# Projecting seven heads of the second batch in float32r passes, with the splits on GpSimd

## The chip, the core and the metric

The program runs on one core of a Trainium2 chip. The metric is the device time of one execution in microseconds. Engines are named as the profile names them: PE is TensorE's matmul, PEld its weight load, DVE is VectorE, ACT is ScalarE, POOL is GpSimd, SP is SyncE, which issues the transfers.

## The reference

A random-feature attention ("performer") over 4 batches, 8 heads, 576 positions and 64 channels is followed by two feed-forward layers on 2304 tokens (512 to 2048 to 512):

```python
proj = np.einsum('bhsd,md->bhsm', x, omega)     # x = q or k, scaled; 128 features
sq = np.sum(x * x, axis=-1, keepdims=True) / 2.0
h = proj - sq
h = h - np.max(h, axis=-1, keepdims=True)
phi = np.exp(h) / np.sqrt(m)
...
kv = np.einsum('bhsm,bhsd->bhmd', k_p, v);  z = np.sum(k_p, axis=2)
num = np.einsum('bhsm,bhmd->bhsd', q_p, kv);  den = np.einsum('bhsm,bhm->bhs', q_p, z)[..., None] + 1e-06
...
h = x @ w_in;  g = h * np.clip(h + 3.0, 0.0, 6.0) / 6.0;  x = g @ w_out      # layer 1
h = x @ w_in;  g = h / (1.0 + np.exp(-1.702 * h));        out = g @ w_out    # layer 2
```

All of it is float32 at the boundary. The first step of the attention, proj, is what the change is about.

## The kernel before, in words

The attention of batch 0 runs alone at the start (to about 45 us). Then layer 1 goes through the batches in four loops of 16 chunks (a chunk is 128 of the 2048 hidden columns): `emit_h` (L506) computes the hidden chunk of one batch, ScalarE and VectorE gate it (L517, L518) and split it (L522, L523), and `emit_o` (L556) multiplies it into the output two chunks later. While batch n goes through its chunks, the attention of batch n+1 is worked in step by step: `att_steps` makes a list of steps, and `side()` takes from it four times in a chunk, at every second call, so that the list is empty at the loop's end. Layer 2 follows from about 560 us (L872, L1003).

Products in layer 1 and 2 are made of float32r passes: an operand is split into a rounded part (hi) and the rest (lo), and three passes hi*hi, hi*lo, lo*hi add up. For a projection this is `project` (L261): `T(h)` splits a head's keys and queries into thi and tlo (L318 a copy, L319 a subtraction, each 128x512, two buffers of either), and `PJ(h, j)` runs 6 passes of 256 columns for the keys (j = 0) and for the queries (j = 1). omega stands in a block-diagonal form in bd_hi and bd_lo, which `factors()` fills with eight small VectorE operations (L699 to L707). The other form is `PJH(h)` (L256): native float32 matmuls of 64 rows and 128 columns on omt, without a split, 8 calls for a head, in two row halves that write two PSUM banks. A flag, `halves`, chooses: before, batches 0 and 1 use PJH (and `PLH` for the 64 positions left over of each head), batches 2 and 3 use T and PJ (and TL, PL). Both forms end in `features`: a maximum over the features on VectorE (L267, from PSUM) and four exponentials on ScalarE (L269). `KV`, `QT`, `NU` and `XT` do the rest of a head on TensorE (L358, L380, L394, L432).

In the first loop (batch 0 in the chunks, batch 1 in the attention) the weights of layer 1 are converted too, one chunk at a time, from the 64-bit words in which they arrive: ScalarE L183 and L185, VectorE L187, L191, L195, GpSimd L200 (two products of 128x512), VectorE L207 (two sums), then the split into hi and lo, ScalarE L210 and VectorE L211. wtop, wmag and wpow, the tiles between these steps, have one buffer each here. The conversion of layer 2's weights follows in the later loops.

The order of the instructions on each engine is made by a scheduler when the program is built: it takes the earliest step of the program that is ready in its own model of time, so an operation that has no one to wait for can come long before its place in the program. On the chip each engine keeps that order.

Of the kernel before, what the change touches and what calls it, by code (L numbers as in the profile page):

```python
# [8 lines left out]
F32 = mybir.dt.float32  # L9
# [6 lines left out]
ALU = mybir.AluOpType  # L16
# [6 lines left out]
def performer_moe_kernel(  # L23
# [13 lines left out]
    nc = tc.nc  # L37
# [5 lines left out]
    H = 2 * NPAIR  # L43
# [60 lines left out]
    def load_pair(b, i):  # L104
        a = at.tile([P, 2, 2, 2, P], F32, tag="qk", bufs=2, name="qk")
        vv = at.tile([P, 2, R, D + 1], F32, tag="v", bufs=2, name="v")
        if (b, i) == (0, 0):
            nc.sync.dma_start(out=a[:, 0], in_=qk[b, i, :, 0])
            nc.sync.dma_start(out=omt, in_=omega)
            load_left(b)  # L110
            nc.sync.dma_start(out=a[:, 1], in_=qk[b, i, :, 1])
        else:
            nc.sync.dma_start(out=a, in_=qk[b, i])
        last_load[0] = nc.sync.dma_start(out=vv, in_=v[b, i])
        qkv[b, i] = (a, vv)

    def load_left(b):
        a = at.tile([P, NPAIR, P], F32, tag="lqk", bufs=1, name="lqk")
        vl = at.tile([P, NPAIR, D + 1], F32, tag="lv", bufs=2, name="lv")
        nc.sync.dma_start(out=a, in_=lqk[b])  # L120
        nc.sync.dma_start(out=vl, in_=lv[b])
        lqkv[b] = (a, vl)
# [31 lines left out]
    def fetch_w(l, k_, c):  # L154
        s = ws_tile(k_, c)
        nc.sync.dma_start(out=s.bitcast(F32), in_=ws_dram[l, k_, c])
        ws[l, k_, c] = s
# [116 lines left out]
    class Att:  # L274


        def __init__(self, b, x, xl, halves=False):
            self.halves = halves
            self.b, self.x, self.xl = b, x, xl
            self.t, self.e, self.kv, self.xt, self.feat, self.qt = {}, {}, {}, {}, {}, {}  # L280

# [33 lines left out]
            self.xln = at.tile([SL, NPAIR, 2, D], F32, tag="xln", name="xln")  # L315

        def split_in(self, hi, lo, a):
            nc.vector.tensor_copy(hi, a)  # L318
            nc.vector.tensor_tensor(out=lo, in0=a, in1=hi.bitcast(F32), op=ALU.subtract)  # L319

        def T(self, h):
            a = qkv[self.b, h // 2][0][:, h % 2]
# [24 lines left out]

        def feature(self, h, j, r):
            e = self.e[h]
            return e[:, r % 2, 2 * j + r // 2] if self.halves else e[:, j, r]  # L350

        def KV(self, h):
            i, p0 = h // 2, 64 * (h % 2)
# [90 lines left out]

    def att_steps(a):
        b = a.b
        st = [] if a.halves else [lambda: a.T(0)]
        for h in range(H + 2):
            if h < H and a.halves:
                st.append(lambda h=h: a.PJH(h))  # L450
            elif h < H:
                st.append(lambda h=h: a.PJ(h, 0))
                st.append(lambda h=h: a.PJ(h, 1))
                if h + 1 < H:
                    st.append(lambda h=h: a.T(h + 1))
            if h == 0:
                st.append(lambda: a.PLH() if a.halves else a.TL())
            if h <= 1 and not a.halves:
                st.append(lambda h=h: a.PL(h))
            if h == 2:  # L460
                st.append(lambda: a.QTL())
            if 2 <= h:
                st.append(lambda h=h: a.NU(h - 2))
            if 1 <= h <= H:
                st.append(lambda h=h: a.QT(h - 1))
                st.append(lambda h=h: a.KV(h - 1))
                if h % 2 == 0:
                    st.append(("load", (h - 1) // 2))
            if 2 <= h and h % 2:
                st.append(lambda h=h: a.XT((h - 2) // 2))  # L470
        st.append(lambda: a.XTL())
        fin = []
        for s in st:
            if isinstance(s, tuple):
                i = s[1] + 2
                bb, i = b + i // NPAIR, i % NPAIR
                if bb < B:
                    prev = fin.pop()

                    def f(prev=prev, bb=bb, i=i):  # L480
                        prev()
                        load_pair(bb, i)
                        if i == 0:
                            load_left(bb)
                    fin.append(f)
            else:
                fin.append(s)
        return fin
# [4 lines left out]
    xblk = {}  # L493
# [96 lines left out]
    def split_x(t, x, kk, eng=nc.gpsimd):  # L590
        nc.scalar.copy(x[:, 0, kk, :], t[:, kk, :])
        eng.tensor_tensor(
            out=x[:, 1, kk, :], in0=t[:, kk, :], in1=x[:, 0, kk, :].bitcast(F32), op=ALU.subtract
        )

    def new_x(i):
        if i == B:
            return lp.tile([P, 2, NK, B * SL], F32R, tag="xl2", name="xl2")
        return xp_.tile([P, 2, NK, SM], F32R, tag="x", bufs=2, name=f"x{i}")
# [85 lines left out]
    for n in range(WARM):  # L685
        nc.tensor.matmul(
            out=ps.rearrange("p a m -> p (a m)"),
# [6 lines left out]
    def factors():  # L694
        for e in range(2):
            o0 = 64 * e
            rows = slice(o0, o0 + 64)
            oth = slice(64 - o0, 128 - o0)
            nc.vector.tensor_copy(bd_hi[rows, e, :], omt[rows, :])  # L699
            nc.vector.tensor_tensor(  # L700
                out=bd_lo[rows, e, :],
                in0=omt[rows, :],
                in1=bd_hi[rows, e, :].bitcast(F32),
                op=ALU.subtract,
            )
            nc.vector.tensor_copy(bd_hi[oth, e, :], zero_r[oth, :].bitcast(F32))
            nc.vector.tensor_copy(bd_lo[oth, e, :], zero_r[oth, :].bitcast(F32))  # L707

    xl = xp_.tile([P, NK, B * SL], F32, tag="xl", name="xl")
    conv = [(l, c) for l in range(2) for c in range(NC)]  # L710
    n_load = [0]
# [2 lines left out]
    def convert_next(stage, upto, act=None, dve=None):  # L714

        while n_conv[stage - 1] < min(upto, len(conv)):
            if stage == 1:
                prefetch_w()
                convert_1(*conv[n_conv[0]], act, dve)
            else:  # L720
                convert_next(1, n_conv[1] + 1, act, dve)
                convert_2(*conv[n_conv[1]])
            n_conv[stage - 1] += 1
        prefetch_w()
# [24 lines left out]
    def before_chunk(n, c):  # L749
        n_late[1] = min(len(late), -(-len(late) * ((n - 1) * NC + c + 1) // slots))  # L750
        late_at("chunk")

    xblk[0] = new_x(0)
    att = Att(0, xblk[0], xl, True)
    steps = att_steps(att)
    for i, st in enumerate(steps):
        if i == len(steps) - TAIL:
# [63 lines left out]
    for u in range(len(units) + LAG):  # L821
        while fetches and fetches[0][0] <= u + AHEAD:
            fetch_w(0, *fetches.pop(0)[1:])
        if u < len(units):
            n, c = units[u]
            if c == 0 and n + 1 < B:
                xblk[n + 1] = new_x(n + 1)
                if n == 1:
                    factors()
                steps = att_steps(Att(n + 1, xblk[n + 1], xl, n == 0))  # L830
                todo = steps[::-1]
                pace[:] = len(todo), 0
            if (n, c) == (B - 2, NC - 1):
                while todo:
                    todo.pop()()
                actx.close()
                lp = ctx.enter_context(
                    tc.tile_pool(name="lp", bufs=1, side="right", reuse_waits="tile")
                )
                xblk[B] = new_x(B)  # L840
                for kk in range(NK):
                    split_x(xl, xblk[B], kk)
            if n > 0:
                before_chunk(n, c)
            emit_h(n, c, side)
            if n == 0:
                convert_next(2, min(c + 2, NC), *(att.feat[H - 1] if c == 0 else ()))
            if (n, c) == (B - 1, PREP):
                assert n_late[0] == len(late)
                prep, _ = x_ops(0, wp, "w")  # L850
            if c == NC - 1:
                while todo:
                    todo.pop()()
        if u >= LAG:
            emit_o(*units[u - LAG], side)
# [343 lines left out]
```

## Time and profile before

| | |
|---|---|
| median of 3 runs | 930.9 us (930.24 to 930.96) |
| the profiled execution | 930.89 us, span 929.1 us |
| PE busy | 914.1 us (98%) |
| DVE busy | 585.9 us (63%) |
| ACT busy | 481.5 us (52%) |
| POOL busy | 334.4 us (36%) |
| TensorE clock granted | 1.0 throughout |

Durations below are those of the profiled execution. Its span counts from the first to the last instruction; 1.8 us of the execution lie around it. The shares are means over stages: in the first loop (36 to 178 us) DVE is much busier than its 63%. Matmuls are pipelined, so the cost of a run of matmuls is read from its first start to the start of what comes next.

### The profile page before, as it was taken

How to read it: one execution, taken by the hardware profiler on the slowest of the kernel's cores; microseconds unless marked ns; L12 is line 12 of the kernel's file. 1: busy time of each engine (PE TensorE's matmuls, PEld its weight loads, DVE VectorE, ACT ScalarE, POOL GpSimd, SP SyncE). 2: the span in 40 equal slices, each digit the busy share in tenths (PEclk: the TensorE clock that was granted, in tenths of full speed). 3: DMA queues.
4: the chain of work that ended last, by engine and by line, in shares of the span. 5: the costliest groups of instructions: out<-in, count | busy, mean ns of one | idle time of the engine just before them, and what ended most of it. 6: DMA issues, size and time to landing. Idle time of an engine off the chain costs nothing.

```text
span 929.1 us, 16457 instructions
## 1 busy us (share of the span) xinstructions
PE 914.1 (98%) x6274; PEld 782.1 (84%) x6274; DVE 585.9 (63%) x980; ACT 481.5 (52%) x977; POOL 334.4 (36%) x283
## 2 busy tenths in 40 slices
PE   8999999999999999999999999999999999999998
PEld 6877777778887888878888888878999888899997
DVE  5888889587585766727643433766875443377653
ACT  6977676476665665636533333444544223244443
POOL 0122222077573547544772112784000244420000
PEclk9999999999999999999999999999999999999999
DMA  6677777889878887766765426999889654566672
GB/s 210 241 250 250 238 248 268 293 297 339 307 271 277 287 319 288 261 238 234 265 239 191 137 93 224 369 405 316 275 285 333 199 175 159 176 187 183 169 261 92
DMA packets 75167, 228.77 MB, mean 246 GB/s; under 512 B 7504, under 2 KB 13264, under 8 KB 75088
## 3 DMA queue, kind: packets, MB, share of 16 engines
q1 hardware_dynamic: 74928, 227.45, 71.2%
q8 instruction: 50, 0.82, 0.3%
q10 hardware_dynamic: 160, 0.26, 0.1%
q14 instruction: 29, 0.24, 0.1%
HBM read 164.77 MB, written 62.91 MB: 245 GB/s over the span
## 4 chain that ended last, share of the span: by engine, by line
PE 84%; DVE 9%; ACT 3%; POOL 2%; issue 1%; DMA 1%; POOLq 0%; DVEq 0%; ACTq 0%
PE o L1003 19%; PE ps L506 18%; PE o L556 18%; PE h L872 16%; PE ps L261 3%; PE hl L889 2%; DVE w L207 2%; PE ps L394 1%; PE ps L256 1%; PE ps L358 1%; DVE gs L523 1%; PE ps L380 1%; POOL w L200 1%; DVE wtop L191 1%; ACT e L269 1%
## 5 line engine op out<-in xcount | busy, mean ns | idle before, releaser
L506 PE MATMUL ps<-x,wss 128*128 128x512 f32 x768 | 193.9, 397 | 3.3 <-ACT wss L210 1.8
L1003 PE MATMUL o<-wss,gs 128*128 128x256 f32 x1536 | 185.4, 283 | 0.3
L1003 PEld LDWEIGHTS o<-wss,gs 128*128 128x128 f32 x1536 | 184.6, 191 | 1.2 <-DVE gs L974 0.5
L506 PEld LDWEIGHTS ps<-x,wss 128*128 128x128 f32 x768 | 139.4, 188 | 35.4 <-ACT wss L210 3.7
L872 PE MATMUL h<-xo,wss 128*128 128x512 f32 x672 | 160.0, 394 | 0.4 <-DVE t L905 0.4
L200 POOL TENSOR_TENSOR w<-w,wpow 128x512 f32<-128x512 f32 x64 | 78.1, 1240 | 202.1 <-DVE wpow L195 123.6
L872 PEld LDWEIGHTS h<-xo,wss 128*128 128x128 f32 x672 | 124.1, 188 | 28.1 <-DVE t L905 0.8
L913 POOL TENSOR_TENSOR g<-g,c 128x512 f32<-128x512 f32 x48 | 64.5, 1346 | 170.3 <-ACT g L912 170.0
L973 ACT CAST gs<-g 128x512 fp32r<-128x512 f32 x112 | 69.4, 621 | 85.1 <-PE o L1003 79.3
L556 PE MATMUL o<-gs,wsh 128*128 128x512 f32 (+1 forms) x480 | 111.7, 377 | 0.3 <-ACT gs L522 0.3
L556 PE MATMUL o<-gs,wss 128*128 128x512 f32 (+1 forms) x480 | 109.4, 374 | 2.4 <-ACT gs L522 2.4
L974 DVE TENSOR_TENSOR gs<-g,gs 128x512 fp32r<-128x512 f32 x112 | 79.7, 716 | 47.8 <-ACT gs L973 45.0
L224 POOL TENSOR_TENSOR wsn<-w,wsn 128x512 fp32r<-128x512 f32 x64 | 90.5, 1429 | 48.8 <-ACT wsn L223 48.8
L518 DVE SCALAR_TENSOR_TENSOR ga<-ga,ps 128x512 f32<-128x512 f32 (+1 forms) x80 | 50.0, 629 | 91.3 <-ACT ga L517 91.1
L517 ACT ACTIVATE ga<-ps,three 128x512 f32<-128x512 f32 (+1 forms) x80 | 51.6, 650 | 94.1 <-PE ps L506 93.9
L556 PEld LDWEIGHTS o<-gs,wss 128*128 128x128 f32 x480 | 81.5, 188 | 17.3 <-ACT gs L522 3.3
L556 PEld LDWEIGHTS o<-gs,wsh 128*128 128x128 f32 x480 | 81.7, 188 | 16.2 <-ACT gs L522 1.0
L269 ACT ACTIVATE e<-ps,mx 128x128 f32<-128x128 f32 x220 | 62.2, 392 | 30.9 <-DVE mx L267 30.9
L523 DVE TENSOR_TENSOR gs<-ga,gs 128x512 fp32r<-128x512 f32 (+1 forms) x80 | 65.1, 824 | 19.4 <-ACT gs L522 18.1
L207 DVE TENSOR_TENSOR w<-w,wtop 128x512 f32<-128x512 f32 x64 | 65.5, 1033 | 10.6 <-POOL w L200 10.2
L912 ACT ACTIVATE g<-c 128x512 f32<-128x512 f32 x48 | 30.3, 632 | 60.3 <-DVE c L905 60.3
L223 ACT CAST wsn<-w 128x512 fp32r<-128x512 f32 x64 | 38.6, 626 | 27.3 <-issue 9.5
(146 smaller groups left out, 1184.1 us busy)
## 6 DMA issues: line engine op xcount, KB each, us to landing
wss<-left SPq DMA_DIRECT2D x64, 512.0 KB, 4.0
wss<-ws0i SPq DMA_DIRECT2D x48, 512.0 KB, 4.6
wraw<-in_w_in_dram SPq DMA_DIRECT2D x32, 512.0 KB, 4.8
wraw<-in_w_out_dram SPq DMA_DIRECT2D x32, 512.0 KB, 5.9
left<-wsn SPq DMA_DIRECT2D x32, 512.0 KB, 3.6
wss<-ws0o SPq DMA_DIRECT2D x24, 512.0 KB, 4.4
ws0i<-wss SPq DMA_DIRECT2D x16, 512.0 KB, 3.1
wss<-sumsa SPq DMA_DIRECT2D x16, 512.0 KB, 3.9
```

What stands on the lines that cost most here:

```text
L200: nc.gpsimd.tensor_tensor(out=w[:, cols], in0=w[:, cols], in1=q[:, cols], op=ALU.mult)
L207: nc.vector.tensor_tensor(out=wj, in0=wj, in1=a[:, j * DM:(j + 1) * DM], op=ALU.add)
L224: nc.gpsimd.tensor_tensor(out=s[:, :, 1], in0=t, in1=s[:, :, 0].bitcast(F32), op=ALU.subtract)
L269: act = nc.scalar.activation(out=e[:, r, :], in_=ps[:, r, :], func=AF.Exp, bias=mx[:, r:r + 1])
L506: nc.tensor.matmul(out=ps, lhsT=w[:, wi, kk, :], rhs=x[:, xi, kk, :], start=(m == 0), stop=(m == 3 * NK - 1),)
L523: gate[1] = nc.vector.tensor_tensor(out=s[:, 1, :], in0=g, in1=s[:, 0, :].bitcast(F32), op=ALU.subtract)
L556: nc.tensor.matmul(out=ps[:, e, :], lhsT=w[:, wi, cols], rhs=s[:, gi, :], start=(c == 0 and m == 0 and per == 1), stop=(c == NC - 1 and m ...
L872: nc.tensor.matmul(out=ps, lhsT=s[:, wi, q, :], rhs=xop[q, op][:, xi], start=(first and m == 0), stop=(m == 5), skip_group_check=not first,)
L913: mul = eng.tensor_tensor(out=g, in0=g, in1=src, op=ALU.mult)
L973: split_ins[0] = nc.scalar.copy(s[:, 0], g)
L974: split_ins[1] = nc.vector.tensor_tensor(out=s[:, 1], in0=g, in1=s[:, 0].bitcast(F32), op=ALU.subtract)
L1003: last_row[0] = nc.tensor.matmul(out=out, lhsT=s[:, gi, d * P:(d + 1) * P], rhs=w[:, wi, :], start=(start and m == 0), stop=(stop and m == 2),
```

## The change

`Att` gets a number, `native`, in place of the flag: so many of its heads use the native form. Batch 0 has all 8, batch 1 has 1 (head 0, and the left-over positions by `PLH` as before), batches 2 and 3 have none, as before. For batch 1 the splits of heads 1 to 7 go to GpSimd; for batches 2 and 3 they stay on VectorE. Since batch 1 now needs bd_hi and bd_lo, `factors()` is called right after omt is scaled and no longer at the start of the second loop. T(h+1) stands in the list of steps behind the projection of head h. Batch 1's list grows from 39 to 53 steps, which `side()` spreads over the same loop.

```diff
-        def __init__(self, b, x, xl, halves=False):
-            self.halves = halves
+        def __init__(self, b, x, xl, native=0, split=None):
+            self.native = native
+            self.split = split or nc.vector
+            self.halves = native > 0
...
         def split_in(self, hi, lo, a):
-            nc.vector.tensor_copy(hi, a)
-            nc.vector.tensor_tensor(out=lo, in0=a, in1=hi.bitcast(F32), op=ALU.subtract)
+            self.split.tensor_copy(hi, a)
+            self.split.tensor_tensor(out=lo, in0=a, in1=hi.bitcast(F32), op=ALU.subtract)
...
         def feature(self, h, j, r):
             e = self.e[h]
-            return e[:, r % 2, 2 * j + r // 2] if self.halves else e[:, j, r]
+            return e[:, r % 2, 2 * j + r // 2] if h < self.native else e[:, j, r]
...
-        st = [] if a.halves else [lambda: a.T(0)]
+        st = [] if a.native else [lambda: a.T(0)]
         for h in range(H + 2):
-            if h < H and a.halves:
+            if h < a.native:
                 st.append(lambda h=h: a.PJH(h))
             elif h < H:
                 st.append(lambda h=h: a.PJ(h, 0))
                 st.append(lambda h=h: a.PJ(h, 1))
-                if h + 1 < H:
-                    st.append(lambda h=h: a.T(h + 1))
+            if a.native <= h + 1 < H:
+                st.append(lambda h=h: a.T(h + 1))
...
+    factors()
+
     xl = xp_.tile([P, NK, B * SL], F32, tag="xl", name="xl")
...
-    att = Att(0, xblk[0], xl, True)
+    att = Att(0, xblk[0], xl, H)
...
-                if n == 1:
-                    factors()
-                steps = att_steps(Att(n + 1, xblk[n + 1], xl, n == 0))
+                steps = att_steps(Att(n + 1, xblk[n + 1], xl, 1 - n if n < 1 else 0, nc.gpsimd if n == 0 else None))
```

## Rows read from the trace of the kernel before

**Rows 1.** Stretches: us, busy time (x instructions) by engine, clock, DMA share, GB/s

```profile
58.00:167.00 109.00, 104.14 (x739) 79.74 (x738) 94.83 (x167) 75.94 (x145) 29.70 (x26) 1.00 0.73 251
...
188.00:313.00 125.00, 124.00 (x853) 100.49 (x852) 90.20 (x149) 76.43 (x171) 76.28 (x65) 1.00 0.85 301
...
313.00:430.00 117.00, 116.87 (x813) 94.39 (x812) 69.06 (x121) 69.34 (x152) 66.29 (x60) 1.00 0.73 255
```

**Rows 2.** Waits, 58 to 167 us: who waits for whom, us, times, longest

```profile
POOL w L200 <- DVE wpow L195: 61.4, 10, 8.2
...
PEld o L556 <- ACT gs L522: 4.3, 6, 1.4
...
PEld ps L506 <- ACT wss L210: 3.4, 4, 1.6
```

**Rows 3.** Timeline, POOL: start, us, engine, line, operation, tiles, count, [idle before]

```profile
103.51 2.30 POOL L200 TENSOR_TENSOR w<-w,wpow 128x512 f32<-128x512 f32 x2 [7.02 <-DVE den L416]
...
110.86 2.28 POOL L200 TENSOR_TENSOR w<-w,wpow 128x512 f32<-128x512 f32 x2 [5.05 <-DVE wpow L195]
...
121.31 2.27 POOL L200 TENSOR_TENSOR w<-w,wpow 128x512 f32<-128x512 f32 x2 [8.18 <-DVE wpow L195]
```

**Rows 4.** Timeline of DVE in the first loop

```profile
104.47 0.69 DVE L518 SCALAR_TENSOR_TENSOR ga<-ga,ps 128x512 f32<-128x512 f32 x1 [0.36 <-ACT ga L517]
...
112.06 1.63 DVE L207 TENSOR_TENSOR w<-w,wtop 128x512 f32<-128x512 f32 x1 [1.34 <-POOL w L200]
...
114.20 0.68 DVE L207 TENSOR_TENSOR w<-w,wtop 128x512 f32<-128x512 f32 x1
```

**Rows 5.** Timeline of PE, native projection of heads 3 and 4, batch 1

```profile
81.88 1.71 PE L256 MATMUL ps<-omt,qk 64*128 64x128 f32 x16
...
83.51 2.57 PE L506 MATMUL ps<-x,wss 128*128 128x512 f32 x10
...
98.41 1.16 PE L256 MATMUL ps<-omt,qk 64*128 64x128 f32 x16
...
99.50 0.68 PE L394 MATMUL ps<-kv,qpt 128*64 128x65 f32 x14
```

**Rows 6.** Timeline of PE, float32r projection of one head, batch 2

```profile
213.47 0.39 PE L261 MATMUL ps<-bd_hi,thi 128*128 128x256 f32 x1
...
214.28 2.91 PE L556 MATMUL o<-gs,wss 128*128 128x512 f32 x12
...
217.03 0.28 PE L261 MATMUL ps<-bd_hi,thi 128*128 128x256 f32 x1
...
217.73 2.91 PE L506 MATMUL ps<-x,wss 128*128 128x512 f32 x12
```

**Rows 7.** Line L224: durations min/median/max in ns, first and last start, form

```profile
L224 POOL TENSOR_TENSOR wsn<-w,wsn x64: 1273/1297/1792, 196.7 to 491.1; 128x512 fp32r<-128x512 f32 x64
```

**Rows 8.** Groups on POOL: busy us, mean ns of one, idle before

```profile
masks.py:199 POOL TENSOR_SCALAR_AFFINE_SELECT ident<-ident 128x128 f32<-128x128 f32 x1 | 0.3, 292 | 0.0
...
masks.py:197 POOL MEMSET ident<- 128x128 f32 x1 | 0.2, 204 | 0.3 <-POOLq L1186 0.3
...
L78 POOL MEMSET three<- 128x1 f32 x1 | 0.1, 99 | 0.0
```

**Rows 9.** Groups on DVE, 36 to 167 us, columns as in rows 8

```profile
L523 DVE TENSOR_TENSOR gs<-ga,gs 128x512 fp32r<-128x512 f32 x14 | 9.4, 680 | 0.0
...
L187 DVE TENSOR_SCALAR wmag<-wtop 128x512 int32<-128x512 int32 x15 | 6.3, 419 | 2.8 <-ACT wtop L183 2.8
```

**Rows 10.** Groups on DVE, 188 to 430 us

```profile
L523 DVE TENSOR_TENSOR gs<-ga,gs 128x512 fp32r<-128x512 f32 x31 | 30.5, 984 | 11.4 <-ACT gs L522 11.3
...
L187 DVE TENSOR_SCALAR wmag<-wtop 128x512 int32<-128x512 int32 x13 | 9.2, 711 | 2.1 <-ACT wtop L183 1.9
```

**Rows 11.** Timeline at the start

```profile
3.93 0.47 DVE L699 CAST bd_hi<-omt 64x128 fp32r<-64x128 f32 x2
```

**Rows 12.** Timeline of ACT in the first loop

```profile
101.69 2.17 ACT L269 ACTIVATE e<-ps,mx 128x128 f32<-128x128 f32 x8
```

## The prediction

> **What bounds the kernel now.** I read first the stretches by stage, then the waits of the first chunk loop, then the order of each engine in it. In the stretch in which batch 0 goes through the chunks (58 to 167 us) TensorE is busy 104.14 of 109 us, so it stands idle for 4.9 us; in the next two loops together it is idle for 1.1 of 242 us [rows 1]. The first loop is thus the one place where TensorE still waits, and the change lies in it. Who makes it wait: the gate's product (L522) and the converted weights (L210, behind L207) [rows 2]. GpSimd's waits say why: in this loop it is nearly always waiting for VectorE's wpow (L195), 61.4 us in 10 waits [rows 2]. The conversion of a chunk's weights is a ring: ScalarE L183, VectorE L187, L191, L195, two GpSimd products L200, two sums L207, and then the next chunk's L183, since wtop, wmag and wpow have one buffer each. Two rounds of it took 103.51 to 110.86 and 110.86 to 121.31 us [rows 3]: the short one has no features in it, the long one has two maxima (L267) and what follows a head. One head falls to about two chunks. In the ring VectorE stops only for the first L200 (1.34 us) [rows 4]. So this loop is held by VectorE's order with the GpSimd step in it, and TensorE comes close behind.
>
> **TensorE: seven projections in another form.** Removed: PJH of heads 1 to 7 of batch 1, 8 calls each, which the trace shows as 16 matmuls. Head 3 took 81.88 to 83.51 = 1.63 us, head 4 took 98.41 to 99.50 = 1.09 us [rows 5]: where the two row halves alternate on the array they run together, otherwise one after the other. By the same view (two of the seven stand there) heads 1 to 7 took some 1.8, 1.50, 1.63, 1.09, 1.09, 1.71 and 1.09, together 9.9 us. Added: PJ, 12 passes of 256 columns for each head; batch 2 shows it in two parts, 213.47 to 214.28 and 217.03 to 217.73, together 1.51 us [rows 6], for seven heads 10.6 us. The sum is +0.7 us; the bounds are 10.6 - 7 x 1.71 = -1.4 us and 10.6 - 7 x 1.09 = +3.0 us. The stage waits for the ring, so I take 0 of it.
> The Trainium skill ("FP8 and Floating Point Precision", TensorE Precision Notes) counts true float32 as four passes through the array. By it a native head would be 8 x 128 x 4 = 4096 columns against 12 x 256 = 3072 of the float32r form, so a quarter of the work would go, an estimate of 0.4 us for each head and 2.9 us in all. Head 4 with its 1.09 us does not bear that out: the two halves overlap there [rows 5].
>
> **GpSimd: seven splits.** T(1) to T(7) each add a copy and a subtraction of 128x512 on GpSimd. The subtraction is the form of L224: 1.27 us at least, 1.30 median [rows 7]. No copy of that size stands in the trace. Upwards, four times the affine select of 128x128 (0.292) gives 1.17 us; downwards, a memset grows from 0.099 for one column to 0.204 for 128, which is 0.52 us at 512 [rows 8]. I take the middle, 0.85. One split is then 2.15 us, seven are 15.0 us (12.6 to 17.3).
> The Trainium skill ("GPSIMD Engine Reference", 3.1 Elementwise) gives 769 ns for a 512-element loop with one input; the sum by it would be 14.4 us.
> GpSimd has room: it is busy 29.70 of 109 us [rows 1]. thi and tlo have two buffers, so a split runs a head ahead of its projection and TensorE does not wait for it (0; a whole split, 2.15 us for each head, if that cover fails).
>
> **What the splits do to VectorE.** This is the term that decides. The first L207 stands beside the second L200 and takes 1.63 us, the second stands alone and takes 0.68 [rows 4]; beside other GpSimd work L523 and L187 grow in the same manner [rows 9, 10], while an operation that reads PSUM keeps its time (L518 at 104.47, 0.69 us beside the pair of 103.51) [rows 3, 4]. So each GpSimd operation that reads SBUF can hold up a VectorE operation with both sides in SBUF until it ends. The price: from 188 to 430 us six groups of this kind (L523, L207, L191, L319, L318, L187) took 33.1 us longer than the same forms in the first loop (the first and the last of the six stand there) [rows 9, 10], with 76.28 + 66.29 = 142.6 us of GpSimd work beside them [rows 1]: 0.23 us for each us of GpSimd. There these groups (with L195) fill 71 of 242 us undisturbed, 29%; from 36 to 167 us they and L211 fill 76 of 131 us, 58%. Twice as likely to meet, so 0.46 us for each us, and 15.0 x 0.46 = 6.9 us more on VectorE. The bounds are 0 (all splits fall beside PSUM reads) and 14 x 0.96 = 13.4 us (each of the 14 operations meets one, as L207 does).
> The Trainium skill ("SBUF — State Buffer", SBUF: two separate sides) speaks against this change: the port pair that both engines use is held for a whole instruction, and the loser blocks fully. By it every meeting would cost up to the whole GpSimd operation, an estimate of 15 us at the worst. The 1.63 us of L207 agrees.
> What of the 6.9 us lies on the path: the ring runs through VectorE's queue, and in a long round, where a head's maxima stand, VectorE does not pause before L187. In a short round L183 leaves a small pause, and TensorE is itself busy for 96% of the loop. I take 0.6 of it: 4.1 us. In the loops after it TensorE is full (124.00 of 125 us, then 116.87 of 117) [rows 1], so what the loop loses comes out at the end.
>
> **Edits at nothing.** factors(): its eight VectorE operations already ran at the start: the four on omt came at 3.93 and then, before the first projection [rows 11]. Moved up in the program they stay there (0; were they ahead of omt's own scaling or of the first maxima, at most the 0.47 us of their two casts and as much again). VectorE's maxima and ScalarE's exponentials keep their number; they come 4 by 4 and not 8 at once. T(0) and T(1) of batch 2, on VectorE, must now wait for thi of heads 6 and 7 of batch 1; they are needed only at 179 us (0). On SP's queue the pairs are loaded after the same KV as before, and the last reader of a pair's keys now comes earlier (0). Of other waits that are added: T(h+1) on GpSimd waits for PJ(h-1) to free thi, and queued behind it is L200 (a rival, below).
>
> **The sum.** 930.9 us in the profiled run (span 929.1 and 1.8 around it), which is the median of the runs as well, + 0 + 4.1 = 935.0 us.
>
> **Rivals.** (a) Faster: the exponentials come in fours. Eight at a stretch held ScalarE for 2.17 us from 101.69, and what the gate needs came behind them [rows 12]; TensorE's weight loads wait 4.3 us for the gate's L522 in the loop [rows 2]. If most of that (3 us) goes, and the projection saves its bound of 1.4 us, with splits beside PSUM reads, the time is about 926.5 us (928 without the projection). Against it: the ring does not become shorter by it. The four-pass count of the Trainium skill would be a part of this case.
> (b) No change: the seven projections are the same work on TensorE, and the splits find the gaps; 931 +- 1.8 us. That is also how it comes out if the change does not do what it says, that is, saves no TensorE time. For it: GpSimd's gaps of 5 to 8 us between the L200 pairs [rows 2, 3]. Against it: in those gaps VectorE is at work on just the forms that collide.
> (c) Slower by more: a split stands in GpSimd's queue ahead of an L200 that is ready, and waits there for PJ two heads earlier. Each such case puts up to 2.15 us on the ring on top of the collisions; with four to seven of them 9 to 15 us, 944 to 950 us. It decides from the point where a split starts later than 2.15 us before L195 ends.
>
> **How the numbers follow.** A measurement of this kernel can tell about 0.2% (1.9 us) from no change. Forecast, slower by 2 to 9 us: 0.39; (a) 0.30; (b) 0.23; (c) 0.08. Most of the chance lies on both sides of zero, so the range reaches from 926.0 (leaving out the far end of (a)) to 942.0 (leaving out (c)); the forecast's own range is 933.0 to 940.0. Faster 0.30, same 0.24, slower 0.46.
>
> **What would show it.** If right: L187, L191, L207, L211 and L523 have higher means between 36 and 167 us, GpSimd is busy some 15 us longer there, the L200 pairs stand further apart in rounds that hold a split, TensorE idles more than 4.9 us in the loop, and from its end on all is shifted. If TensorE's idle time shrinks and L522 waits less, it is (a). If L200 waits behind a split, (c). The forecast is wrong if VectorE's means stay as they are although the splits ran, or if they grow and the L200 pairs keep their distance.

## The result and the profile after

The changed kernel takes 937.6 us (936.9 to 938.1, four runs) against 930.6 us (930.1 to 931.0, four runs) beside it: ratio 1.0075, interval 1.0062 to 1.0087. It is slower by 7.0 us, and the forecast was 935.0 us in a range of 926 to 942. The profiled execution took 936.9 us. In the changed file the lines of `emit_h`, `emit_o`, the gate and the heads stand two lower (L506 is L508, L523 is L525, L318 and L319 are L320 and L321); L183 to L211, L256, L261 and L267 keep theirs.

The page's head and busy time of TensorE, kernel after:

```profile
span 935.1 us, 16429 instructions
PE 914.4 (98%) x6246; PEld 784.2 (84%) x6246; DVE 594.5 (64%) x980; ACT 483.0 (52%) x977; POOL 350.2 (37%) x297
```

A span is TensorE's busy time and its idle time. Before it was 914.1 + 15.0 = 929.1 us, after it is 914.4 + 20.7 = 935.1 us: TensorE is not busy longer, it stands idle 5.7 us longer. Where, the stretches tell (columns as in [rows 1]); the first line is of the kernel before, the others of the kernel after, and the first two of these are the first loop:

```profile
36.00:58.00 22.00, 21.58 (x184) 16.05 (x184) 19.23 (x43) 20.62 (x53) 4.55 (x4) 1.00 0.78 270
...
36.00:58.00 22.00, 18.99 (x171) 14.06 (x171) 20.08 (x43) 19.81 (x47) 8.34 (x8) 1.00 0.75 270
58.00:167.00 109.00, 101.69 (x658) 80.21 (x657) 93.77 (x158) 75.00 (x142) 38.43 (x34) 0.97 0.69 238
188.00:313.00 125.00, 124.00 (x854) 100.45 (x853) 90.50 (x150) 76.77 (x167) 75.02 (x64) 1.00 0.85 301
313.00:430.00 117.00, 116.87 (x818) 94.67 (x817) 69.95 (x122) 69.01 (x158) 63.55 (x56) 1.00 0.75 263
```

From 58 to 167 us TensorE is busy 101.69 us where it was 104.14 [rows 1]; from 36 to 58 us it is 18.99 where it was 21.58. So 5.0 of the 5.7 us of idle time lie in the first loop. The two later stretches agree with [rows 1] to the hundredth. From 58 to 167 us also the granted clock, the first column behind POOL's, is 0.97 and no longer 1.00.

The waits of the same stretch, 58 to 167 us, kernel after (columns as in [rows 2]):

```profile
POOL w L200 <- DVE wpow L195: 55.7, 11, 8.4
...
PEld ps L508 <- ACT wss L210: 8.0, 5, 2.3
...
PEld o L558 <- ACT gs L524: 1.6, 1, 1.6
```

TensorE's weight loads now wait 1.6 us for the gate where it was 4.3, and 8.0 us for converted weights where it was 3.4 [rows 2]. So the wait that rival (a) wanted gone did shrink by 2.7 us, and another grew by 4.6.

What the splits cost on their own engine and on VectorE: groups on POOL, 28 to 130 us, and on DVE, 36 to 167 us, kernel after, with the line of L207 of the kernel before behind them (columns as in [rows 8]):

```profile
L321 POOL TENSOR_TENSOR tlo<-qk,thi 128x512 fp32r<-128x512 f32 x7 | 10.7, 1533 | 0.4
L320 POOL CAST thi<-qk 128x512 fp32r<-128x512 f32 x7 | 5.0, 710 | 43.2 <-DVE mx L267 28.5 <-PE ps L261 11.4 <-DMA qk<-in_qk_dram 3.4
```

```profile
L207 DVE TENSOR_TENSOR w<-w,wtop 128x512 f32<-128x512 f32 x28 | 32.8, 1176 | 9.3 <-POOL w L200 9.3
...
L525 DVE TENSOR_TENSOR gs<-ga,gs 128x512 fp32r<-128x512 f32 x14 | 10.9, 779 | 0.9 <-ACT gs L524 0.8
L191 DVE SCALAR_TENSOR_TENSOR wtop<-wtop,wmag 128x512 int32<-128x512 int32 x15 | 10.8, 720 | 0.2
...
L187 DVE TENSOR_SCALAR wmag<-wtop 128x512 int32<-128x512 int32 x15 | 6.5, 433 | 1.3 <-ACT wtop L183 1.1
```

```profile
L207 DVE TENSOR_TENSOR w<-w,wtop 128x512 f32<-128x512 f32 x30 | 32.7, 1102 | 10.0 <-POOL w L200 9.8
```

A split takes 0.71 + 1.53 = 2.24 us, seven 15.7 us. The means of L525 and L187 were 680 and 419 ns [rows 9]; L207's was 1102 and, by the same view of before, L191's 687. So VectorE did get slower, by 28 x 0.074 + 14 x 0.099 + 15 x 0.033 + 15 x 0.014 = 4.2 us in these four groups.

Now the order of it. GpSimd's timeline, a pair of L200 in the middle of the loop and the last rounds of the ring, kernel after, and behind it two of these pairs in the kernel before; the columns are start, duration, engine, line, operation, and in brackets the idle time before it and who ended that:

```profile
114.33 2.28 POOL L200 TENSOR_TENSOR w<-w,wpow 128x512 f32<-128x512 f32 x2 [2.27 <-DVE rden L422]
...
124.78 1.75 POOL L321 TENSOR_TENSOR tlo<-qk,thi 128x512 fp32r<-128x512 f32 x1
130.57 2.28 POOL L200 TENSOR_TENSOR w<-w,wpow 128x512 f32<-128x512 f32 x2 [4.04 <-DVE wpow L195]
138.57 2.35 POOL L200 TENSOR_TENSOR w<-w,wpow 128x512 f32<-128x512 f32 x2 [5.73 <-DVE wpow L195]
147.61 2.28 POOL L200 TENSOR_TENSOR w<-w,wpow 128x512 f32<-128x512 f32 x2 [6.70 <-DVE wpow L195]
158.27 2.60 POOL L200 TENSOR_TENSOR w<-w,wpow 128x512 f32<-128x512 f32 x2 [8.38 <-DVE wpow L195]
166.31 1.16 POOL L200 TENSOR_TENSOR w<-w,wpow 128x512 f32<-128x512 f32 x1 [5.44 <-DVE wpow L195]
```

```profile
138.13 2.29 POOL L200 TENSOR_TENSOR w<-w,wpow 128x512 f32<-128x512 f32 x2 [7.02 <-DVE wpow L195]
...
161.63 2.28 POOL L200 TENSOR_TENSOR w<-w,wpow 128x512 f32<-128x512 f32 x2 [4.66 <-DVE wpow L195]
```

The last split on GpSimd ends at 126.5 us. In the kernel before the last four pairs came at 138.13, 145.65, 154.69 and 161.63. So the pair of 138.57 is late by 0.44 us, with all seven splits behind it, and the last one by 4.68 us, with none of them in between. That looks as if the splits did not touch the ring, but the rounds do not hold the same work. The pair at 114.33 stands where the kernel before has that of 110.86 [rows 3], so it is late by 3.47 us. From the ring's second pair up to there VectorE runs the same 107 operations in both kernels; stretches, kernel before and kernel after:

```profile
41.78:110.86 69.08, 67.31 (x488) 51.73 (x488) 59.25 (x107) 52.89 (x111) 18.29 (x17) 1.00 0.72 244
```

```profile
41.79:114.33 72.54, 67.16 (x457) 52.03 (x454) 63.37 (x107) 53.24 (x108) 27.78 (x24) 0.98 0.70 241
```

VectorE is busy for 63.37 us with them, where it was 59.25. So in these rounds the same operations take it 4.1 us longer, and the ring comes 3.5 us late, which fits the prediction (how much of it the splits make, e1 asks below). The delay shrinks to 0.44 us behind them because VectorE puts work off: its splits of heads 0 and 1 of batch 2 stood at 118.2 to 120.8 us in the kernel before, and now, since heads 6 and 7 of batch 1 hold the tiles thi and tlo until their projections, they come at 138.3, 142.0, 156.8 and 158.0 us. These 2.2 us lie in the last rounds now.

What else holds these is seen at 147 to 156 us. VectorE's and TensorE's timelines, kernel after:

```profile
152.79 0.43 DVE L187 TENSOR_SCALAR wmag<-wtop 128x512 int32<-128x512 int32 x1
154.97 0.69 DVE L267 TENSOR_REDUCE mx<-ps 128x4 f32<-128x512 f32 x1 [1.75 <-PE ps L261]
155.57 0.68 DVE L191 SCALAR_TENSOR_TENSOR wtop<-wtop,wmag 128x512 int32<-128x512 int32 x1
```

```profile
148.18 1.07 PE L558 MATMUL o<-gs,wss 128*128 128x512 f32 x4
151.15 0.73 PE L508 MATMUL ps<-x,wss 128*128 128x512 f32 x2 [1.90 <-ACT wss L210]
151.81 1.13 PE L360 MATMUL ps<-v,e 128*64 128x65 f32 x16
152.87 0.48 PE L368 MATMUL ps<-lv,el 64*64 64x65 f32 x4
153.28 0.58 PE L261 MATMUL ps<-bd_hi,thi 128*128 128x256 f32 x1
```

TensorE has come to L508 before the weights of that chunk are converted and stands for 1.90 us; KV (L360) and the last projection (L261), which ask for other data, stand behind it. VectorE has the maximum of that projection (L267) queued ahead of the ring's L191, and waits 1.75 us for it. Part of that wait is the clock: this projection takes 2.37 us, where five others took 1.36 to 1.52, and it runs at half the clock, as the next lines show. The round took 10.66 us, the longest of those that begin at 41.79 us or later.

And the clock, stretches after the two longest such gaps (1.89 us up to 99.67 and 1.90 us up to 151.15), kernel after:

```profile
98.00:102.00 4.00, 2.33 (x24) 1.73 (x25) 3.96 (x10) 3.00 (x5) 0.42 (x1) 0.82 0.57 226
102.00:106.00 4.00, 4.00 (x17) 3.31 (x16) 2.75 (x8) 2.21 (x5) 1.10 (x1) 0.75 0.87 240
...
150.00:154.00 4.00, 2.85 (x25) 2.25 (x26) 3.21 (x6) 3.39 (x6) 0.00 (x0) 0.72 0.02 6
154.00:158.00 4.00, 4.00 (x22) 3.59 (x21) 3.03 (x6) 1.80 (x5) 0.00 (x0) 0.85 1.04 332
```

In the clock records these are two stretches of 3.41 us at half the clock, 1.2 GHz for 2.4; each takes up to 1.7 us of work. The kernel before has none in this loop: its longest gaps there, 1.19 and 1.21 us, were not followed by one.

### The profile page after: what moved, and what is told of

Same layout as the page of the kernel before. It is cut to its first block, busy times and chain, and to the rows that moved or that the text cites. A ratio compares the mean times of both kernels' runs of the same rounds, so it can differ in the third digit from the quotient of the medians.

```text
span 935.1 us, 16429 instructions
## 1 busy us (share of the span) xinstructions
PE 914.4 (98%) x6246; PEld 784.2 (84%) x6246; DVE 594.5 (64%) x980; ACT 483.0 (52%) x977; POOL 350.2 (37%) x297
## 4 chain that ended last, share of the span: by engine, by line
PE 81%; DVE 10%; ACT 3%; POOL 2%; issue 2%; DMA 1%; POOLq 0%; SPq 0%; DVEq 0%; ACTq 0%
PE o L1005 19%; PE o L558 17%; PE ps L508 17%; PE h L874 14%; DVE w L207 3%; PE ps L261 3%; PE hl L891 2%; POOL w L200 1%; PE ps L396 1%; PE ps L360 1%; DVE gs L525 1%; DVE mx L267 1%; PE ps L382 1%; DVE wtop L191 1%; DMA fac<-xf 1%
## 5 line engine op out<-in xcount | busy, mean ns | idle before, releaser
L508 PE MATMUL ps<-x,wss 128*128 128x512 f32 x768 | 194.8, 398 | 8.9 <-ACT wss L210 6.4
L508 PEld LDWEIGHTS ps<-x,wss 128*128 128x128 f32 x768 | 139.8, 189 | 41.9 <-ACT wss L210 9.5
L200 POOL TENSOR_TENSOR w<-w,wpow 128x512 f32<-128x512 f32 x64 | 78.9, 1253 | 148.1 <-DVE wpow L195 121.2
L224 POOL TENSOR_TENSOR wsn<-w,wsn 128x512 fp32r<-128x512 f32 x64 | 90.4, 1428 | 48.8 <-ACT wsn L223 48.8
L525 DVE TENSOR_TENSOR gs<-ga,gs 128x512 fp32r<-128x512 f32 (+1 forms) x80 | 67.1, 849 | 20.1 <-ACT gs L524 18.7
L207 DVE TENSOR_TENSOR w<-w,wtop 128x512 f32<-128x512 f32 x64 | 68.5, 1077 | 11.3 <-POOL w L200 11.1
L524 ACT CAST gs<-ga 128x512 fp32r<-128x512 f32 (+1 forms) x80 | 46.1, 581 | 12.2 <-DVE ga L520 12.1
```

The costliest lines, as they stand in the source:

```text
L200: nc.gpsimd.tensor_tensor(out=w[:, cols], in0=w[:, cols], in1=q[:, cols], op=ALU.mult)
L207: nc.vector.tensor_tensor(out=wj, in0=wj, in1=a[:, j * DM:(j + 1) * DM], op=ALU.add)
L224: nc.gpsimd.tensor_tensor(out=s[:, :, 1], in0=t, in1=s[:, :, 0].bitcast(F32), op=ALU.subtract)
L508: nc.tensor.matmul(out=ps, lhsT=w[:, wi, kk, :], rhs=x[:, xi, kk, :], start=(m == 0), stop=(m == 3 * NK - 1),)
L525: gate[1] = nc.vector.tensor_tensor(out=s[:, 1, :], in0=g, in1=s[:, 0, :].bitcast(F32), op=ALU.subtract)
```

## The experiments

The texts of what was expected speak of theories by letters. A is the prediction: the splits hold up VectorE, and with it the ring. B: the order around the new projection, with a maximum ahead of a step of the ring, as just shown. C: another cut of the list of steps is enough, whatever the steps do, since it changes where the scheduler puts everything. D: a finer list brings the first heads later, which shows as idle time at 36 to 58 us. E: every order but the one of before costs some microseconds.

All were timed beside the kernel before, whose medians were 930.6 to 930.8 us. "Busy" and "idle" are TensorE's over the whole span of the profiled execution, "ring" is the time from the second to the last pair of L200 in the first loop, "half" the stretches at half the clock in that loop and, for the two with `side()` moved, the one behind it. The profiled execution is one of those timed and lies up to 2.7 us from the median (e3, profiled at 937.6 us), so these columns go with it and not with the median.

| kernel | median us | ratio, interval | busy + idle | half, us | ring |
|---|---|---|---|---|---|
| before | 930.6 | | 914.1 + 15.0 | none | 119.9 |
| after | 937.6 | 1.0075 (1.0062 to 1.0087) | 914.4 + 20.7 | 3.41, 3.41 | 124.5 |
| e1, no splits | 936.9 | 1.0060 (1.0040 to 1.0081) | 916.2 + 20.4 | 6.83, 3.41 | 125.8 |
| e2, splits on VectorE | 936.2 | 1.0053 (1.0036 to 1.0070) | 915.0 + 19.6 | 3.41 | 124.3 |
| e3, native and splits | 940.3 | 1.0102 (1.0069 to 1.0135) | 915.6 + 20.2 | 3.41 | 123.3 |
| e4, 16 empty steps | 938.5 | 1.0080 (1.0063 to 1.0096) | 920.2 + 17.8 | 6.83, 3.41 | 123.6 |
| e5, after in 39 steps | 938.4 | 1.0086 (1.0071 to 1.0101) | 916.2 + 19.6 | 3.41, 3.41 | 121.2 |
| e6, e3 in 39 steps | 941.0 | 1.0114 (1.0099 to 1.0130) | 918.3 + 22.5 | 3.41, 6.83 | 130.1 |
| e7, factors() early | 930.6 | 1.0001 (0.9991 to 1.0011) | 913.9 + 15.8 | none | 120.3 |
| e8, steps 4 calls early | 936.4 | 1.0065 (1.0050 to 1.0080) | 918.4 + 17.2 | two | 121.8 |
| e9, one empty step | 934.2 | 1.0040 (1.0025 to 1.0055) | 917.1 + 15.2 | 6.83 | 121.8 |
| e10, two wtop | 936.1 | 1.0061 (1.0046 to 1.0076) | 915.1 + 20.7 | 3.41 | 97.5 |
| e11, after, two wtop | 937.8 | 1.0077 (1.0062 to 1.0092) | 914.7 + 21.3 | 6.83, 3.41 | 99.4 |
| e12, after, 4 calls early | 944.8 | 1.0162 (1.0141 to 1.0183) | 916.5 + 25.3 | three | 128.5 |

**The splits taken away (e1) and moved (e2).** In the changed kernel, batch 1's heads 2 to 7 read head 1's split:

```diff
+            if self.native and h > 1:
+                self.t[h] = self.t[1]
+                return
```

> The changed kernel without the splits of heads 2 to 7 of batch 1: their projections read the split tiles of head 1 (so these heads are projected from head 1's data), the projection stays in float32r passes. Theory A (the prediction: GpSimd's splits hold up VectorE in the ring of the weight conversion): the loss is gone, 931 +- 2 us, waits of TensorE for the converted weights (L210) fall from 5.9 us back to about 2 us in the loop. Theory B (the order around the new projection: VectorE's maximum of a half head stands in its queue ahead of the ring's next step and waits for TensorE, which itself waits for the ring's weights): 935 to 938 us, as the changed kernel. Theory C (any other order of the same work would do it, since the list of steps is longer and is cut in another way): 935 to 938 us as well.

It took 936.9 us, 0.7 us less than the changed kernel (1.4 us by the ratios), and the intervals overlap. The waits of 58 to 167 us and a VectorE group of 36 to 167 us, kernel e1 (L508 is L511 here):

```profile
PEld ps L511 <- ACT wss L210: 8.1, 6, 2.3
...
PE ps L511 <- ACT wss L210: 5.6, 6, 1.9
```

```profile
L207 DVE TENSOR_TENSOR w<-w,wtop 128x512 f32<-128x512 f32 x28 | 31.9, 1142 | 12.4 <-POOL w L200 12.4
```

TensorE waits for converted weights as long as with all the splits (8.1 against 8.0), its idle time is 20.4 us against 20.7, and more than half of L207's growth (1102 to 1142, of 1102 to 1176) is there as well. One of seven splits and 2.3 us of GpSimd's work are left. The ring is no shorter either: the pair of L200 that came at 114.33 comes at 115.67 us here, and from the second pair up to it VectorE is busy for 62.48 us with the same operations and one split of its own (0.43 + 1.33 us). So 1.5 of the 4.1 us are there without GpSimd's splits. So idle time of this size and a ring as late do not need the splits. What part the splits had in the changed kernel this run does not tell, since it has another order again.

Then the splits given back to VectorE:

```diff
-                steps = att_steps(Att(n + 1, ..., nc.gpsimd if n == 0 else None))
+                steps = att_steps(Att(n + 1, ..., None))
```

> The changed kernel with the splits of batch 1 on VectorE. They take 0.41 + 0.68 = 1.1 us there for each head, 7.7 us in all, where GpSimd's cost VectorE about 5 us of blocked time. Theory A: the ring runs through VectorE, so 934 to 940 us, no better than the changed kernel. Theory B: the splits matter little wherever they are, 935 to 939 us. If it falls to 931 us, it is GpSimd itself that costs (its queue, not VectorE's time).

936.2 us: 1.5 us less than with GpSimd (2.0 us by the ratios, the intervals overlap), though VectorE now does seven splits more itself. Which engine makes the splits is worth little here. The result lies in the ranges of both theories.

**The splits alone (e3, e6).** The kernel before, its native projections kept, with seven splits on GpSimd that nobody reads; in e3 as steps of their own (46 in the list), in e6 within the projection's step (39, as before):

```diff
                 st.append(lambda h=h: a.PJH(h))
+                if b == 1 and h + 1 < H:
+                    st.append(lambda h=h: a.T2(h + 1))     # e6: in one lambda with PJH(h)
```

> The kernel before with the seven splits added on GpSimd and read by no one: projections stay native. Theory A: 933 to 937 us, the cost of the splits alone. Theories B and C: 931 +- 1 us, since the projection and its order are those of before (the list of steps is 7 longer).

> The kernel before with the seven unread splits on GpSimd, now each within the step of a native projection: 39 steps as before. Theory D: 930 to 932 us. Theory A: 934 to 938 us. Theory E: 934 to 940 us.

940.3 us and 941.0 us, the slowest but for one, and above every range that was given for them. Alone these two would speak for A, at more than its price. But the four executions of e3, in one and the same order, took 937.6 and 938.4 us at a granted clock of 0.998, and 942.1 and 944.3 us at 0.990 and 0.991: its median rests on the two with the lower clock. And they stand beside the next two.

**The list cut otherwise (e4, e9).** The kernel before with steps that do nothing, two behind each projection of batch 1 (55 steps), and then a single one (40 steps):

```diff
                 st.append(lambda h=h: a.PJH(h))
+                if b == 1:
+                    st.extend([lambda: None] * 2)
...
+                if b == 1 and h == 0:                      # e9
+                    st.append(lambda: None)
```

> The kernel before with two empty steps behind each projection of batch 1, so that the list of steps is cut as finely as in the changed kernel (55 steps for 39; changed: 53). Nothing is computed in another way. Theories A and B: 931 +- 1.5 us. Theory C (a different cut of the same work is enough): 934 us or more.

> The kernel before with one empty step behind the first projection of batch 1 (40 steps for 39). Theory E (each other order of this work costs some us, because the order before happens to keep TensorE fed): 934 to 939 us, with idle stretches of over 1.2 us on TensorE in the first loop and a stretch at half clock behind at least one of them. If the loss grows with the number of steps (D, in a weaker form): 930.6 to 931.5 us.

The empty steps cost 7.8 us and the single one 3.4 us. No operation is added, no split, no form is changed; only `side()` hands out the steps at other calls, and the scheduler sets another order. e9 is the cleanest case in the study, since its idle time is that of before (15.2 against 15.0 us) and nearly all of the loss is busy time (917.1 against 914.1). Stretches and TensorE's timeline, kernel e9:

```profile
54.00:56.00 2.00, 2.00 (x6) 1.23 (x5) 1.35 (x3) 2.00 (x4) 0.00 (x0) 0.50 0.48 193
56.00:58.00 2.00, 2.00 (x9) 1.71 (x8) 0.45 (x1) 1.50 (x2) 0.00 (x0) 0.50 0.91 256
```

```profile
51.87 0.77 PE L508 MATMUL ps<-x,wss 128*128 128x512 f32 x2 [1.10 <-ACT x L250]
53.09 2.42 PE L508 MATMUL ps<-x,wss 128*128 128x512 f32 x6 [0.45 <-DVE x L251]
55.44 2.07 PE L256 MATMUL ps<-omt,qk 64*128 64x128 f32 x8
57.44 3.99 PE L508 MATMUL ps<-x,wss 128*128 128x512 f32 x10
61.36 1.16 PE L256 MATMUL ps<-omt,qk 64*128 64x128 f32 x8
```

Behind gaps of 1.10 and 0.45 us the granted clock is 0.50. Ten matmuls of L508 take 3.99 us, where ten took 2.57 in [rows 5], and eight of L256 take 2.07 us at 55.44 and 1.16 at 61.36, after the clock came back. In the records the stretch is 6.83 us long, up to 3.4 us of lost work; the span grew by 3.2 us. E had the time right, but had looked for the fall behind a gap of over 1.2 us; these two are shorter. C holds in its plainest form: a re-ordering that changes no work costs 3.4 us, half of what the change cost.

**The change in the old list (e5).** The changed kernel with a head's projection and split merged into one step, 39 steps as before:

```diff
+            if a.native == 1 and h < H:
+                own = [st.pop() for _ in range(...)][::-1]
+                st.append(lambda own=own: [s() for s in own])
```

> The changed kernel with each head's projection (both halves) and the next head's split put into one step, so that batch 1's list has 39 steps again, in the same program order. Theory D (the finer list: a head's steps take more of side()'s calls, the first heads come later, TensorE idles and its clock falls around 36 to 58 us): 929 to 932 us, TensorE idle under 1 us from 36 to 58 us. Theory A (GpSimd's splits on top of that): 933 to 936 us. Theory E (each order the scheduler makes other than the one before is some us worse, whatever is changed): 934 to 939 us, with idle time in other places.

938.4 us, the same as in 53 steps. A list of the old length does not give the old order back, since other instructions stand in it. The idle time at 36 to 58 us is still there (busy 19.16 of 22 us, 18.99 in the changed kernel), though the list is no finer than before, so D is not the cause of it. From 58 to 167 us TensorE is even busier than in the kernel before (106.37 against 104.14 us), and the loss has moved to 185 to 430 us (241.75 of 245 against 243.88).

**factors() alone (e7).** The kernel before with only that call moved:

```diff
+    factors()
+
     xl = xp_.tile([P, NK, B * SL], F32, tag="xl", name="xl")
...
-                if n == 1:
-                    factors()
```

> The kernel before with only factors() moved to the start. Its eight operations already ran there, the list of steps is untouched. Theories A and D: 930.5 +- 1 us. Theory E: it moves too, by 2 us or more, since the order on TensorE differs in some places though no work does.

930.6 us, ratio 1.0001: it costs nothing, as A and D had it. E had expected another order on TensorE, but there is none: on each engine the trace has the same instructions in the same sequence as the kernel before, which no other run here has on TensorE. So e7 is no test of E. It shows that the same order gives the same time.

**The same list, handed out earlier (e8, e12).** `side()` takes each step four calls earlier, in the kernel before (e8) and in the changed one (e12):

```diff
-    while todo and (pace[0] - len(todo)) * 4 * NC < pace[0] * pace[1]:
+    while todo and (pace[0] - len(todo)) * 4 * NC < pace[0] * (pace[1] + 4):
```

> The kernel before with side() four calls ahead in its count in every loop: each list's first steps come earlier and it is empty a chunk sooner. Theory D: the first heads come earlier, so no idle time from 36 to 58 us, 928 to 932 us, about as before or a little better. Theory E: 933 to 939 us.

> The changed kernel with side() four calls ahead in its count, so that the first heads of each list come earlier. Theory D (late first heads): 929 to 933 us. Theory E: 934 to 940 us, as the kernel before with the same shift (936.4 us).

936.4 us and 944.8 us; the second lies above either theory's range. In e8 TensorE idles less in the first loop, busy 146.17 of 149 us from 36 to 185 us against 143.72 (up to 1.7 us of the difference is work at half the clock), and more in the loops behind it, 239.83 of 245 us from 185 to 430 us against 243.88. So the order of before is not the one with the least idle time in the first loop; it leaves no hole behind it. e12 has the same hole behind the loop (239.15 of 245), and the changed kernel's own on top.

**The ring made shorter (e10, e11).** Two buffers for wtop, so that a chunk's L183 need not wait for the last sum of the chunk before; in the kernel before (e10) and in the changed one (e11):

```diff
-    tag=f"wtop{l and c % 2}"
+    tag=f"wtop{c % 2}"
```

> The kernel before with two buffers for wtop in the conversion of layer 1's weights, so that the next chunk's L183 need not wait for L207. If the ring of the conversion holds the first loop (theory A's ground): 925 to 929 us. If it doesn't, or if the order decides (E): 930 to 938 us.

> The changed kernel with two buffers for wtop. If the ring holds the loop and the splits lengthen it (A): 930 to 934 us, most of the loss is back. If the order decides (E): 935 to 940 us, no clear gain over the changed kernel's 937.6 us.

This is the run that asks whether the ring bounds the loop. GpSimd's timeline, the second and the last pair of L200, kernel e10:

```profile
42.24 2.77 POOL L200 TENSOR_TENSOR w<-w,wpow 128x512 f32<-128x512 f32 x2 [9.50 <-ACT kv L374]
...
139.76 3.06 POOL L200 TENSOR_TENSOR w<-w,wpow 128x512 f32<-128x512 f32 x2 [6.22 <-ACT w L185]
```

It ends 21.9 us before that of the kernel before (161.63), and the kernel is 5.3 us slower than it: TensorE idles 5.7 us longer and has a stretch at half the clock, where the kernel before has none. Its gaps have moved, from the converted weights to the attention; TensorE's timeline, kernel e10:

```profile
125.37 0.65 PE L380 MATMUL ps<-ident,e 128*128 128x128 f32 x4 [1.83 <-DVE wtop L191]
...
135.42 1.12 PE L432 MATMUL ps<-ident,xt 128*128 128x128 f32 x4 [2.21 <-DVE den L416]
```

In the changed kernel the same edit shortens the ring from 124.5 to 99.4 us and moves the time by 0.2 us (937.8 against 937.6). A ring that is 22 to 25 us shorter thus does not shorten the loop in either kernel. These edits draw a new order too, so what the ring alone is worth they do not tell. Ahead of the den at 135.3 us, for which TensorE waits, two steps of the ring (L207 and L187, 134.0 and 134.6 us) stand in VectorE's queue.

## Why the prediction was right, and why its reason was not

**Sign, size and range: right.** 937.6 us lies 2.6 us above the forecast, in the forecast's own range of 933 to 940 us. That was in part luck: no run ties the 7.0 us to the reason that was given, as the next points show.

**TensorE's work, +0.7 us: near.** Five of the seven float32r projections took 1.36 to 1.52 us in the trace of after, as [rows 6] had it, the first in its two parts 1.86 us with a wait of 0.23 in it, and that of 153.28 took 2.37 us at half the clock. The native ones of [rows 5] had been counted at 9.9 us for seven. TensorE's busy time is 914.4 against 914.1 us. That sum has the two half-clock stretches in it, up to 3.4 us, so some 3 us of other busy time must have gone. A part of it can be named: in the groups of TensorE's instructions over the whole execution, the native projections of left-over positions (L256 into ps from lqk, 24 matmuls) are busy for 2.2 us after and 3.6 before, and those of batch 0 into acc (72 matmuls) for 10.0 and 10.8. These are the same instructions in another order. Where the rest went is not settled; busy time counts modelled ends.

**GpSimd's splits, 15.0 us: right.** 15.7 us; the copy took 0.61 us undisturbed and 0.71 in the mean (0.85 assumed between 0.52 and 1.17), the subtraction 1.28 and 1.53 us (1.30 assumed). The Trainium skill ("GPSIMD Engine Reference", 3.1 Elementwise) has 769 ns for a tight loop over 512 elements; the 0.61 us of the copy lies under it. The prediction's sum by it, 14.4 us, comes to 14.5.

**Collisions on VectorE, 6.9 us: right in kind, too large.** The four groups above grew by 4.2 us, and with the wsh half of L211 (840 against 685 ns, seven times) by 5.3. But e1, without the splits, has L207 at 1142 ns and the gate's product at 745: 28 x 0.040 + 14 x 0.065 = 2.0 us of the 5.3 came from the order and not from splits. Some 3 us are left for them. The price was read too high as well: of the 33.1 us, 7.6 are L207's, counted against its undisturbed 0.68 us (24 x 0.318), but its mean was 1102 ns in the first loop and 998 behind it, so it did not grow. The Trainium skill ("SBUF — State Buffer", SBUF: two separate sides) lets the loser of the port pair that both engines share block fully; the rows agree that operations grow, and at 15.7 us of GpSimd work the price in the mean was 0.2 to 0.3 us for each, far from the 15 us that the prediction gave for the worst case.

**"0.6 of it on the path", 4.1 us: this step failed, in its second half.** It said that what VectorE loses lengthens the ring, and that the ring's end is the loop's end. The first fits the changed kernel's trace: up to the pair of 114.33 VectorE was busy 4.1 us longer for the same operations (1.5 of it in e1 as well), and the ring was 3.5 us late. The second does not hold. Without six of the seven splits TensorE's idle time and the 6 us stay (e1), with a ring 25 us shorter the changed kernel takes the same time (e11), and with one 22 us shorter the kernel before gets slower (e10). The row from which I took the bound, GpSimd's 61.4 us of waiting for wpow [rows 2], tells how long the ring is and who is next in it. That TensorE waits at its end it did not tell; only 3.4 us of TensorE's own waits did [rows 2]. The prediction had named as a sign against it that the L200 pairs keep their distance. Over the eleven rounds from 41.79 to 138.57 us, in which five of the seven splits run (the first two run before), the ring takes 96.78 us against 96.35 before; but the splits of batch 2, put off until later, are in the one and not in the other, so this sign does not decide.

**Edits at nothing.** The splits of heads 0 and 1 of batch 2, which must wait for thi, were put at 0 since they are needed only at 179 us. They moved into the last rounds of the ring, 2.2 us on VectorE. Whether that reached the end, no run here tells.

**In its place.** The program's order on the queues was redrawn, and TensorE ran dry at a few places where a matmul that waits stands ahead of others that do not, such as the 1.90 us up to 151.15. The idle time grew by 5.7 us, and two stretches at half the clock followed. By e4, e8 and e9 edits that leave the work as it is cost 3.4 to 7.8 us in the same kernel, so the change's 7.0 us lies within what a re-ordering costs. That the time went into such gaps and clock stretches is shown by the traces. That an order alone can make them is shown by the runs that change nothing else, and e7, which keeps the order, keeps the time. That it was the order in the changed kernel too is inferred: no run has the change in the order of before. The order does not fix all of it, either: e1 took 934.8 us at a granted clock of 0.999 and 938.4 at 0.994. Two things stay open. Why the order of before is the good one was not found: e8 idles less in the first loop and more behind it. And the share of the splits: 0.7 us by after against e1, while e3 and e6 (940.3 and 941.0) lie 2 to 7 us above the neutral edits (934.2 to 938.5). Those differ in order too, e3's median has the clock in it, and no run here parts these.

**Rivals.** (a): the weight loads' wait for the gate fell from 4.3 to 1.6 us, near the 3 us it claimed, and the wait for weights took it back. That the exponentials in fours did it is not shown: from 58 to 167 us this wait is 4.4 us in e2, which has them in fours, and 1.1 us in e3 and 1.4 us in e6, which have them in eights. (b) was right about TensorE's work and silent on the order. (c) did not happen: of the pairs of L200 only the first, at 30.35, starts straight behind a split's copy, and it starts earlier than in the kernel before (31.03); all others start after a pause. That a different order of everything is itself a case with a price stood nowhere among the rivals, though the prediction knew that a scheduler sets the order and that the list grows from 39 to 53 steps.

## What to carry to other kernels

Where a scheduler or a list of steps sets the order, time one edit that does nothing (an empty step, a shift) before an operation is credited or blamed: here that floor was 3.4 to 7.8 us, as large as the effect, and a single run with a split or without it would have proved either story. Compare rounds of a loop only where they hold the same operations. A long cycle of waits on engines other than TensorE is no bound until a run that shortens it gains; e10 shortened it by 22 us and lost. And read the granted clock behind each idle gap of TensorE: in e9 its stretch of 6.83 us is enough for the whole loss.

## What the runs showed of the hardware

In a kernel that keeps TensorE busy for 98% of its span, the clock fell from 2.4 to 1.2 GHz behind gaps of one or two microseconds: for 3.41 us each behind gaps of 1.89 and 1.90 us in the changed kernel, and for 6.83 us behind gaps of 1.10 and 0.45 us close together in e9. It did not fall behind gaps of 1.19 and 1.21 us in the kernel before, nor behind one of 1.66 us up to 118.21 in the changed one, nor behind one of 2.83 us up to 111.84 in e3 (granted clock 1.00 from 104 to 120 us), so the length of a gap alone does not tell it. In e9 ten matmuls that took 2.57 us before took 3.99, most of it at half the clock. A gap of 1.9 us thus cost its own length and up to 1.7 us more.

One program, in one order, can also get another share of the clock from one execution to the next: e3 took 937.6 us at a granted clock of 0.998 and 944.3 us at 0.991.
